# Decay attention, then two MLPs, on one core: the inverted row sums transposed into the banks of the value products, and ScalarE copying all four groups of transposed probabilities

## The chip, the cores and the metric

One core of one Trainium2 chip runs the whole kernel in one launch. The metric is the device time in microseconds (us), the median of three runs. Engines are named as in the profile: PE is TensorE (PEld its weight loads), DVE VectorE, ACT ScalarE, POOL GpSimd, SP the queue that issues most DMAs. Each engine works through its own queue in program order, so an instruction that waits holds up everything queued behind it on that engine.

## What is computed

Causal attention with a decay bias over 4 x 8 heads, 576 tokens, head size 64, and two MLPs behind it on the 2304 tokens:

```python
scores = scale * np.matmul(q, k.transpose(0, 1, 3, 2))
cum = np.cumsum(np.maximum(s, 0.0), axis=-1)
bias = -(cum[:, :, :, None] - cum[:, :, None, :])
scores = np.where(causal, -1000000000.0, scores + np.minimum(bias, 0.0))
scores = scores - np.max(scores, axis=-1, keepdims=True)
attn = np.exp(scores)
attn = attn / (np.sum(attn, axis=-1, keepdims=True) + 1e-09)
x = np.matmul(attn, v)                      # rearranged to 2304 x 512
x = np.maximum(x @ moe_w_in, 0.0) ** 2 @ moe_w_out
h = np.maximum(np.maximum(x @ w1, x @ w2), x @ w3)
return h @ moe2_w_out
```

## The kernel before

**Attention.** The 32 heads are worked in 16 pairs; the two heads of a pair sit in the two halves of the 128 partitions. Each pair has NU = 9 *units* u = 0 to 8: units 0 to 7 are 64-row blocks of queries (two units share a matmul group of 128 query rows, and unit u has (u // 2 + 1) x 128 keys), unit 8 is the tail of 64 queries with 576 keys. Units 0 to 3 are window w = 0, units 4 to 8 window w = 1. A unit goes through these steps:

- `s` (u_s, PE): scores of a pair of units into one of two score tiles; `max` (u_max, DVE): adds the causal bound, takes the negated maximum; `exp` (u_exp, ACT): exponentials, with the row sums accumulated into `sums[p, w]`.
- `t` (u_t, PE, L727): 64 x 64 transposes of the probabilities into a tile of `ring_t`; done at odd units (units 1 and 3 share a tile) and at unit 8, so there are four groups, here t3, t5, t7 and t8.
- `et` (u_et): each group is copied to SBUF: et3 (L754), et5 and et7 (L756) by ACT, et8 (L759) by DVE.
- `pv` (w_pv, PE, L779): the value products of a window into another tile of `ring_t`; pv0 needs et3, pv1 needs et5, et7 and et8. `out0`/`out1` (w_out_, DVE, L787) copies the product to SBUF.
- `rc` (w_rc, DVE, L695 and L696): adds 1e-9 to the window's sums and inverts them. Two small transposes (PE, L734) bring them into columns 448 to 511 of the tile of t5 (window 0) or t8 (window 1), and `cp` (w_cp, DVE, L690) copies them out.
- `keep` (SP, L702, L704) stores these rows in DRAM, `rows` (SP, L711) reads them back broadcast over 64 partitions, `px` (POOL, L792) multiplies, `xst` (SP, L797) stores the result in `x_at`.

`ring_t` has two tiles of two banks, taken in turn: t3, t5 and t7 of a pair fall on one, pv1 of the pair before, pv0 and t8 on the other. So t7 waits until t5's tile has been read, t8 until pv0's has, and pv1 until t8's has.

**The order of the work.** `attention()` runs a step number n over all 144 units; in each step it goes through ORDER and does operation `op` for unit n + d. The list is the order of each engine's queue. `pump` starts or continues the preparation of MLP weights (loads L392 on SP; L397 to L408 on DVE; L415 and L433 on POOL; L429 on ACT) in six of nine steps. Before the operations of a step come the loads of later pairs: k, q and the cumulated sums at unit 7, v at unit 6 of a pair. In step numbers modulo 9, PE's queue is

```
t7 s2 t8 [sums of w=1] s4 t3(u=1) s6 pv1 t3(u=3) s8 t5 [sums of w=0] s0(next pair) pv0
```

where t7, t8 and pv1 belong to the pair before the one whose scores are being made.

**The MLPs.** `experts()` follows on the same queues. The first MLP goes over eight blocks of the hidden dimension per visit of a token chunk: h products (L810), relu, square and a split into two parts (ACT L973 to L975, DVE L976), and the x products (L997) two blocks behind. For the next chunk it loads `x_at` (SP, L900) and splits it (ACT L802, DVE L805). In this stage the weight loads L392 are issued on POOL.

Of the kernel before, what the change touches and what calls it, by code (L numbers as in the profile page):

```python
# [8 lines left out]
F32 = mybir.dt.float32  # L9
# [40 lines left out]
ST_BUFS = 3  # L50
PACE = 1.5
PACE_ATT = 5
ORDER = [("rc", -2), ("max", 1), ("cp", -3), ("out0", -6), ("out1", -7), ("exp", -1), ("et", -3), ("t", -2), ("s", 2), ("pv", -5), ("rows", -13),
         ("pump", 0), ("keep", -6), ("px", -19), ("xst", -21)]

# [189 lines left out]
def kernel(  # L247
# [15 lines left out]
    nc = tc.nc  # L263
    P = 128
    D = v_tail.shape[2]
# [11 lines left out]
    NU = 2 * SQ // P + 1  # L277
    U0 = 4
# [19 lines left out]
    def psum(at, name, n, shape, side="left"):  # L298
        ps = at.enter_context(tc.tile_pool(name=name, bufs=1, side=side, space=PSUM, reuse_waits="tile"))
        return [ps.tile(shape, F32, name=f"{name}{i}") for i in range(n)]  # L300
# [212 lines left out]
    keep = {i: dram.tile([P, 1024], F32, name="keep_" + "_".join(map(str, i))) for i in second + late}  # L513
# [10 lines left out]
    small = phA.enter_context(tc.tile_pool(name="small", bufs=6))  # L524
# [7 lines left out]
    identF = at1.tile([P, P], F32, name="identF")  # L532
# [16 lines left out]
    def rows(j):  # L549
        return slice(D * j, D * j + D)  # L550
# [68 lines left out]

    NP = MAX_PAIRS or BH // 2  # L620
    units = [(p, u) for p in range(NP) for u in range(NU)]
    wins, ends = {}, {}
    for n, (p, u) in enumerate(units):
        if u in (U0 - 1, NU - 1):
            wins[n] = (p, int(u >= U0))
        if u in (U0 + 1, NU - 1):
            ends[n] = (p, int(u == NU - 1))
    st = {}
    s_t = {}
    t_t = {}  # L630
# [39 lines left out]
    sums = {}  # L670
# [8 lines left out]
        nc.scalar.activation(out=e_u[u][:, 0:w], in_=e_u[u][:, 0:w], func=ACTF.Exp, scale=-1.0, bias=st.pop(n),  # L679
                             accum_out=sums[p, win][:, col:col + 1])  # L680

    tr_t = {}
    rs_t = {}
    rec_t = {}


    def w_cp(p, w):
        nu = U0 + w
        sm = small.tile([NU - U0, P], F32, tag="rec", name="rec", bufs=2)
        nc.vector.tensor_copy(sm[0:nu, :].rearrange("u (h c) -> u h c", c=D), tr_t.pop((p, w)))  # L690
        rec_t[p, w] = sm

    def w_rc(p, w):
        sm = sums[p, w][:, 0:U0 + w]
# [20 lines left out]
    def u_t(n):  # L715
        p, u = units[n]
        b = u // 2
        if u == NU - 1:
            blocks = [(u, k, k) for k in range(NKT)]
        elif u % 2:  # L720
            blocks = [(u - 1 + j, k, (k + (b == 1)) * 2 + j) for k in range(b + 1) for j in range(2)]
        else:
            return
        t = t_t[n] = t_t.pop(n - 2) if u == U0 - 1 else ring_t.take()
        for v, k, at in blocks:
            for h in range(2):
                nc.tensor.transpose(t[:, h, at * D:(at + 1) * D], e_u[v][rows(h), k * P:(k + 1) * P], identF[rows(h), rows(h)])  # L727

        if n in ends:
            _, w = ends[n]  # L730
            o = tr_t[p, w] = t[0:U0 + w, :, 7 * D:8 * D]
            sm = sums.pop((p, w))
            for h in range(2):
                nc.tensor.transpose(o[:, h, :], sm[rows(h), 0:U0 + w], identF[rows(h), rows(h)])  # L734

    et_t = {}

    def u_et(n):
        p, u = units[n]
        if u == U0 - 1:  # L740
            et = et_t[p, 0] = et_p.tile([P, 2, 3, 2, D], F32, tag="et0", name="et0")
            m = 6
        elif u > U0 and (u % 2 or u == NU - 1):
            if u == U0 + 1:
                et_t[p, 1] = et_p.tile([P, NKT, 2, W1 // D, D], F32, tag="et1", name="et1")
            et = et_t[p, 1]
            m = NKT if u == NU - 1 else u + 1
            at = (u - U0) & ~1
        else:
            return  # L750
        t = t_t.pop(n)
        src = t[:, :, 0:m * D]
        if u < U0:
            nc.scalar.copy(out=et.rearrange("p h b j c -> p h (b j c)"), in_=src)  # L754
        elif u < NU - 1:
            nc.scalar.copy(out=et[:, 0:m // 2, :, at:at + 2, :].rearrange("p k j h c -> p h k j c"),  # L756
                           in_=src.rearrange("p h (k j c) -> p h k j c", j=2, c=D))
        else:
            nc.vector.tensor_copy(et[:, :, :, at, :].rearrange("p k j c -> p j k c"),  # L759
                                  src.rearrange("p j (k c) -> p j k c", c=D))  # L760
        ring_t.give(t)

    pvt = {}
# [1 line left out]
    def w_pv(p, w):  # L765
        t = pvt[p, w] = ring_t.take()
        pv = t[:, 0, :]
        xv = hd[p]["xv"]
        et = et_t.pop((p, w))
        last = (2, NKT)[w] - 1  # L770
        for k in range(last + 1):
            kr = ST if k == 4 else P
            f = max(0, k * P - W0 * w)
            for j in range(2):
                if w:
                    rhs = et[0:kr, k, j, f // D:, :]
                else:
                    rhs = (et[:, :, 0:2, j, :] if k == 0 else et[:, :, 2:3, j, :]).rearrange("p h b c -> p b h c")
                nc.tensor.matmul(pv[rows(j), f:(W0, W1)[w]], lhsT=xv[0:kr, j, k, :], rhs=rhs, start=(k == 0), stop=(k == last))  # L779

    ax_t = {}

    def w_out_(p, w):
        t = pvt.pop((p, w))
        n = (W0, W1)[w]
        x = ax_t[p, w] = ax_p.tile([P, W1], F32, tag="ax", name="ax")
        nc.vector.tensor_copy(x[:, 0:n], t[:, 0, 0:n])  # L787
        ring_t.give(t)

    def w_px(p, w):  # L790
# [28 lines left out]
    def first_split(kk, step):  # L819
        t0, n = chunks1[0]  # L820
        if step == 0:
            fx[kk] = fx_p.tile([P, 512], F32, tag="fx", name="fx")[:, 0:n]
            nc.sync.dma_start(out=fx[kk], in_=x_at[kk, :, t0:t0 + n])
        elif step == 1:
            first_x[kk] = tuple(slots_a[-1 - kk][:, i, :] for i in range(2))
            high(fx[kk], first_x[kk][0][:, 0:n])
        else:
            low_of(fx[kk], first_x[kk][0][:, 0:n], first_x[kk][1][:, 0:n])

    def first_products():  # L830
        for m in range(PRE):
            yield from h_products(banks[m], first_x, chunks1[0][1], slots.get(("in", m)))

    def attention():
        setup()
        for f in loads(1):
            f()
        N = len(units)
        fns = dict(s=u_s, t=u_t, max=u_max, et=u_et, exp=u_exp)
        efn = dict(cp=w_cp)  # L840
        wfn = dict(rc=w_rc, pv=w_pv, out0=w_out_, out1=w_out_, keep=w_keep, rows=w_rows, px=w_px, xst=w_xst)
        span = max(abs(d) for _, d in ORDER)
        pre = first_products()
        coming = {}
        for n in range(-span, N + span + 1):
            if 0 <= n < N:
                p = n // NU
                for back in range(3):
                    if p + 2 - back < NP and p >= back:
                        to = p + 2 - back  # L850
                        if n == (to - 2) * NU + LOADS[0]:
                            coming[to] = loads(to)
                        for at, f in zip(LOADS, coming.get(to, ())):
                            if n == (to - 2) * NU + at:
                                f()
            for op, d in ORDER:
                if op == "pump":
                    if PUMP_FROM <= n < N + PUMP_END and n % NU in PUMP_U and (slots.free or slots.open):
                        slots.pump(1)
                elif op in efn:  # L860
                    if n + d in ends:
                        efn[op](*ends[n + d])
                elif op in wfn:
                    if n + d in wins and op not in ("out1", "out0")[wins[n + d][1]]:
                        wfn[op](*wins[n + d])
                elif 0 <= n + d < N:
                    fns[op](n + d)
            if n == N - PRE_AT:
                phQ.close()
                banks.extend(psum(ctx, "first", 2, [P, 512]))  # L870
            for kk in range(KD):
                for step, off in enumerate((-8, 0, 1)):
                    if n == N - PRE_X[kk] + off:
                        first_split(kk, step)
            if n >= N - PRE_AT:
                for _ in range(PRE_N):
                    next(pre, None)
        for _ in pre:
            pass
# [277 lines left out]
    with tc.manual_schedule():  # L1157
        attention()
        phA.close()
        phP.close()  # L1160
        banks.extend(psum(ctx, "banks", 6, [P, 512], "right"))
        if not ONLY_ATT:
            experts()
# [55 lines left out]
```

## Time and profile before

| | |
|---|---|
| time, median of 3 runs | 858.42 us (858.33 to 860.21) |
| the profiled execution: its time / its span | 858.48 us / 856.7 us |
| busy over the span | PE 97%, PEld 82%, DVE 63%, ACT 47%, POOL 18% |
| attention, 40 to 170 us: busy of 130 us | PE 118.3, DVE 105.3, ACT 100.0, POOL 40.9 |
| one pair of heads in attention, from one t7 to the next | 10.36 us where nothing else disturbs it |
| MLPs, from about 188 us to the end | PE busy throughout |

The span is what the profiler records of one execution; the time lies 1.8 us above it. Rows are read as: start and length in us, engine, line, operation, tile written <- tile read, and in square brackets how long the engine stood idle before it and what ended that.

### The profile page before, as it was taken

Reading aid. Unit: us, or ns where it says so; the run is one execution under the profiler, and the core shown is the slowest. Engines: PE = TensorE matmul, PEld = TensorE weight load, DVE = VectorE, ACT = ScalarE, POOL = GpSimd, SP = SyncE. Lnnn points to the kernel's source line nnn. Section 1 sums busy time; section 2 is a strip of 40 time slices with the busy share of each in tenths; the row PEclk is TensorE's granted clock in tenths of the full one; section 3 lists DMA queues with packets and bytes.
Section 4 is the critical chain, followed back from the end, with each engine's and each line's share of the span. In section 5 each row is a group of like instructions: output and inputs, shape, how many; then the busy total and the mean of one; then the engine's idle time right before and its main releaser. Section 6 shows DMA issues by size and latency. Waiting matters only on the chain.

```text
span 856.7 us, 14331 instructions
## 1 busy us (share of the span) xinstructions
PE 827.8 (97%) x5284; PEld 702.1 (82%) x5284; DVE 539.9 (63%) x1119; ACT 401.5 (47%) x817; POOL 155.6 (18%) x237
## 2 busy tenths in 40 slices
PE   5999899899999999999999999999999999999998
PEld 3555555568888889999998888889998899989996
DVE  6787888758885657577677876753464335623442
ACT  5777778764544455445554454442233122421222
POOL 2032323334112332214222314100000000000000
PEclk9999999999999999999999999999999999999999
DMA  4555556635344644698658677719940674026601
GB/s 136 175 157 172 185 179 184 190 98 182 109 174 140 222 168 142 235 394 281 204 190 306 227 268 252 249 74 390 405 152 13 208 249 144 14 74 198 244 1 73
DMA packets 72245, 159.75 MB, mean 186 GB/s; under 512 B 11376, under 2 KB 31408, under 8 KB 72176
## 3 DMA queue, kind: packets, MB, share of 16 engines
q1 hardware_dynamic: 56916, 107.45, 37.0%
q0 software_dynamic: 15248, 51.39, 17.4%
q8 instruction: 41, 0.67, 0.3%
q14 instruction: 28, 0.23, 0.1%
q10 hardware_dynamic: 12, 0.01, 0.0%
HBM read 113.53 MB, written 45.27 MB: 185 GB/s over the span
## 4 chain that ended last, share of the span: by engine, by line
PE 91%; DVE 4%; ACT 2%; DMA 2%; issue 1%; SPq 0%; ACTq 0%; DVEq 0%
PE banks L997 23%; PE banks L1134 13%; PE first L810 12%; PE banks L810 12%; PE banks L1106 9%; PE first L1134 8%; PE pairs L779 4%; PE pairs L727 4%; PE pair L642 2%; PE pairs L642 2%; ACT et L756 1%; PE pair L649 1%; PE pairs L649 1%; DVE e L665 1%; DVE hh L805 1%
## 5 line engine op out<-in xcount | busy, mean ns | idle before, releaser
L997 PE MATMUL banks<-hh,sl 128*128 128x512 f32 (+1 forms) x960 | 209.9, 367 | 0.0
L997 PEld LDWEIGHTS banks<-hh,sl 128*128 128x128 f32 x960 | 175.2, 188 | 22.6
L1134 PE MATMUL banks<-xs,sl 128*128 128x384 f32 x702 | 131.2, 335 | 0.0
L1134 PEld LDWEIGHTS banks<-xs,sl 128*128 128x128 f32 x702 | 122.8, 188 | 0.9 <-DMA sl<-keep_p 0.2
L976 DVE TENSOR_TENSOR hh<-r,hh 128x512 fp32r<-128x512 f32 (+1 forms) x80 | 52.0, 651 | 98.4 <-ACT hh L975 98.2
L810 PE MATMUL first<-xs,sl 128*128 128x512 f32 (+1 forms) x432 | 93.6, 365 | 0.0
L810 PE MATMUL banks<-xs,sl 128*128 128x512 f32 (+1 forms) x432 | 93.6, 365 | 0.0
L679 ACT ACTIVATE e<-e,nm 128x128 f32<-128x128 f32 (+2 forms) x144 | 83.3, 582 | 15.6 <-DVE nm L665 15.2
L810 PEld LDWEIGHTS first<-xs,sl 128*128 128x128 f32 x432 | 78.6, 188 | 9.4
L810 PEld LDWEIGHTS banks<-xs,sl 128*128 128x128 f32 x432 | 78.6, 188 | 9.4
L1134 PE MATMUL first<-xs,sl 128*128 128x384 f32 x432 | 84.6, 335 | 0.3 <-DMA sl<-keep_p 0.3
L1106 PE MATMUL banks<-sl,hh 128*128 128x512 f32 (+1 forms) x342 | 78.4, 382 | 1.9 <-DVE hh L805 1.5
L1134 PEld LDWEIGHTS first<-xs,sl 128*128 128x128 f32 x432 | 75.8, 188 | 0.9 <-issue 0.6
L1106 PEld LDWEIGHTS banks<-sl,hh 128*128 128x128 f32 x342 | 61.4, 188 | 15.9 <-DVE hh L805 3.4
L973 ACT ACTIVATE r<-banks 128x512 f32<-128x512 f32 (+1 forms) x40 | 22.2, 556 | 95.0 <-PE banks L810 91.5
L973 ACT ACTIVATE r<-first 128x512 f32<-128x512 f32 (+1 forms) x40 | 22.2, 556 | 90.7 <-PE first L810 90.7
L727 PEld LDWEIGHTS pairs<-identF,e 64*128 64x128 f32 x800 | 34.0, 141 | 28.1 <-ACT et L756 20.9
L727 PE MATMUL pairs<-identF,e 64*128 64x64 f32 x800 | 41.8, 232 | 14.2 <-ACT et L756 14.2
L1035 ACT COPY s<-first 128x384 f32<-128x384 f32 x36 | 17.2, 479 | 79.3 <-PE first L1134 79.2
L779 PEld LDWEIGHTS pairs<-et,xv 128*64 128x64 f32 (+1 forms) x448 | 27.8, 135 | 31.2 <-issue 5.9
L779 PE MATMUL pairs<-et,xv 128*64 128x320 f32 (+4 forms) x448 | 52.7, 367 | 0.0
L1035 ACT COPY s<-banks 128x384 f32<-128x384 f32 x45 | 21.6, 479 | 57.5 <-PE banks L1134 56.7
(105 smaller groups left out, 1155.5 us busy)
## 6 DMA issues: line engine op xcount, KB each, us to landing
sl<-keep_p SPq DMA_DIRECT2D x68, 512.0 KB
st<-in_w_dram POOLq DMA_DIRECT2D x36, 256.0 KB, 6.0
st<-in_w_out_dram POOLq DMA_DIRECT2D x35, 256.0 KB, 3.8
sl<-keep_out SPq DMA_DIRECT2D x14, 512.0 KB
keep_p<-hi POOLq DMA_DIRECT2D x9, 768.0 KB, 4.9
keep_p<-sums POOLq DMA_DIRECT2D x9, 768.0 KB, 6.5
st<-in_w_in_dram POOLq DMA_DIRECT2D x22, 256.0 KB, 4.1
xr<-x_at SPq DMA_DIRECT2D x20, 256.0 KB
```

What stands on the lines that cost most here:

```text
L642: nc.tensor.matmul(b[:, j, 0:w], lhsT=d["xq"][rows(j), w - P:w], rhs=d["xk"][rows(j), 0:w], start=True, stop=False)
L649: nc.tensor.matmul(b[rows(j), i, 0:hi - lo], lhsT=d["xq"][rows(j), SQ:S], rhs=d["xk"][rows(j), lo:hi], start=True, stop=False)
L679: nc.scalar.activation(out=e_u[u][:, 0:w], in_=e_u[u][:, 0:w], func=ACTF.Exp, scale=-1.0, bias=st.pop(n), accum_out=sums[p, win][:, col:co ...
L727: nc.tensor.transpose(t[:, h, at * D:(at + 1) * D], e_u[v][rows(h), k * P:(k + 1) * P], identF[rows(h), rows(h)])
L779: nc.tensor.matmul(pv[rows(j), f:(W0, W1)[w]], lhsT=xv[0:kr, j, k, :], rhs=rhs, start=(k == 0), stop=(k == last))
L810: nc.tensor.matmul(hps[:, 0:n], lhsT=w[:, wp, kk * P:(kk + 1) * P], rhs=x[kk][xp][:, 0:n], start=(kk == 0 and c == 0), stop=(kk == KD - 1 ...
L973: nc.scalar.activation(out=r[:, 0:n], in_=hps[:, 0:n], func=ACTF.Relu)
L976: nc.vector.tensor_tensor(out=hh[:, 1, 0:n], in0=r[:, 0:n], in1=f32(hh[:, 0, 0:n]), op=ALU.subtract)
L997: nc.tensor.matmul(xacc[d][:, 0:n], lhsT=w[:, wp, d * P:(d + 1) * P], rhs=hh[:, xp, 0:n], start=(m == 0 and c == 0), stop=(end and c == 2))
L1035: nc.scalar.copy(out=x, in_=bank[:, 0:T2])
L1106: nc.tensor.matmul(b, lhsT=hh[g, t][:, hp_, q, h, :], rhs=w[:, wp, lo:hi], start=(begin and n == h == c == 0), stop=(end and n == len(f) - ...
L1134: nc.tensor.matmul(at[m, b][:, 0:T2], lhsT=w[:, wp, at_w + kk * P:at_w + (kk + 1) * P], rhs=x[:, kk, xp, :], start=(i in (0, 1, 3) and kk ...
```

## The change

Three things move. The transposes of the inverted sums leave u_t and stand at the end of w_pv, into columns 448 to 511 of the tile of the value products; `cp` disappears as a step and its copy follows `out` in w_out_. The copy of the fourth group (et8) goes from DVE to ACT. In ORDER `rc` goes two steps later and behind `max`, and `keep`, `rows`, `px` and `xst` go two steps later. The buffers of the copied sums (`rec`) go from 2 to 4.

```diff
-ORDER = [("rc", -2), ("max", 1), ("cp", -3), ("out0", -6), ("out1", -7), ("exp", -1), ("et", -3), ("t", -2), ("s", 2), ("pv", -5), ("rows", -13),
-         ("pump", 0), ("keep", -6), ("px", -19), ("xst", -21)]
+ORDER = [("max", 1), ("rc", -4), ("out0", -6), ("out1", -7), ("exp", -1), ("et", -3), ("t", -2), ("s", 2), ("pv", -5), ("rows", -15),
+         ("pump", 0), ("keep", -8), ("px", -21), ("xst", -23)]
...
-    def w_cp(p, w):
-        nu = U0 + w
-        sm = small.tile([NU - U0, P], F32, tag="rec", name="rec", bufs=2)
-        nc.vector.tensor_copy(sm[0:nu, :].rearrange("u (h c) -> u h c", c=D), tr_t.pop((p, w)))
-        rec_t[p, w] = sm
...
-        if n in ends:
-            _, w = ends[n]
-            o = tr_t[p, w] = t[0:U0 + w, :, 7 * D:8 * D]
-            sm = sums.pop((p, w))
-            for h in range(2):
-                nc.tensor.transpose(o[:, h, :], sm[rows(h), 0:U0 + w], identF[rows(h), rows(h)])
...
-            nc.vector.tensor_copy(et[:, :, :, at, :].rearrange("p k j c -> p j k c"),
-                                  src.rearrange("p j (k c) -> p j k c", c=D))
+            nc.scalar.copy(out=et[:, :, :, at, :].rearrange("p k j c -> p j k c"),
+                           in_=src.rearrange("p j (k c) -> p j k c", c=D))
...
                 nc.tensor.matmul(pv[rows(j), f:(W0, W1)[w]], lhsT=xv[0:kr, j, k, :], rhs=rhs, start=(k == 0), stop=(k == last))
+        sm = sums.pop((p, w))
+        for h in range(2):
+            nc.tensor.transpose(t[0:U0 + w, h, 7 * D:8 * D], sm[rows(h), 0:U0 + w], identF[rows(h), rows(h)])
...
         nc.vector.tensor_copy(x[:, 0:n], t[:, 0, 0:n])
+        sm = rec_t[p, w] = small.tile([NU - U0, P], F32, tag="rec", name="rec", bufs=4)
+        nc.vector.tensor_copy(sm[0:U0 + w, :].rearrange("u (h c) -> u h c", c=D), t[0:U0 + w, :, 7 * D:8 * D])
         ring_t.give(t)
```

## Rows read from the trace of the kernel before

**Rows 1.** The page's head.

```profile
span 856.7 us, 14331 instructions
```

**Rows 2.** Busy us (instructions) in a stretch: PE, PEld, DVE, ACT, POOL; clock; DMA; GB/s.

```profile
40.00:170.00 130.00, 118.32 (x1436) 70.66 (x1432) 105.34 (x363) 99.99 (x268) 40.89 (x42) 0.99 0.59 177
```

**Rows 3.** Waits, 10 to 190 us: who waited for whom: total us, times, longest.

```profile
PE pairs L727 <- ACT et L756: 14.2, 15, 1.7
...
ACT et L754 <- PE pairs L727: 18.6, 15, 1.8
...
ACT et L756 <- DVE rec L690: 10.8, 14, 1.4
```

**Rows 4.** Timeline of one pair that nothing else disturbs.

```profile
71.14 0.71 PE L727 MATMUL pairs<-identF,e 64*128 64x64 f32 x16 [0.69 <-ACT et L756]
...
79.19 0.76 DVE L665 CUSTOM_DVE_ANT_0 e<-pairs,bound_l 128x576 f32<-128x576 f32 x1 [0.88 <-PE pairs L652]
...
79.94 0.87 PE L779 MATMUL pairs<-et,xv 128*64 128x256 f32 x8
...
80.29 0.27 DVE L690 COPY rec<-pairs 4x128 f32<-4x128 f32 x1
...
80.65 0.80 ACT L756 COPY et<-pairs 128x768 f32<-128x768 f32 x1 [0.66 <-DVE rec L690]
...
80.91 0.42 DVE L787 COPY ax<-pairs 128x256 f32<-128x256 f32 x1
...
81.50 0.71 PE L727 MATMUL pairs<-identF,e 64*128 64x64 f32 x16 [0.69 <-ACT et L756]
...
82.65 0.47 PE L727 MATMUL pairs<-identF,e 64*128 64x64 f32 x10
...
83.40 0.40 ACT L679 ACTIVATE e<-e,nm 128x128 f32<-128x128 f32 x1
...
83.75 0.80 DVE L759 COPY et<-pairs 128x640 f32<-128x640 f32 x1
...
85.28 2.42 PE L779 MATMUL pairs<-et,xv 128*64 128x320 f32 x20
```

**Rows 5.** Groups by line and shape: count | busy, mean ns.

```profile
L695 DVE TENSOR_SCALAR sm<-sm 128x4 f32<-128x4 f32 x16 | 8.3, 517 | 0.0
...
L696 DVE RECIPROCAL sm<-sm 128x4 f32<-128x4 f32 x16 | 2.9, 178 | 0.6
```

**Rows 6.** Timeline: one of the sums' instructions beside POOL.

```profile
86.95 1.23 POOL L415 TENSOR_TENSOR wa<-st 128x512 f32<-128x512 f32 x1
...
87.20 1.01 DVE L695 TENSOR_SCALAR sm<-sm 128x4 f32<-128x4 f32 x1
```

**Rows 7.** The same view behind the longest of these waits; 0.66 is the clock.

```profile
156.00:161.00 5.00, 4.31 (x46) 3.30 (x48) 3.08 (x12) 4.21 (x12) 0.04 (x1) 0.66 0.59 189
```

**Rows 8.** Timeline of SP's queue: a window-1 keep and the next one.

```profile
77.46 0.62 SPq L702 DMA_DIRECT2D r<-rec  x1
...
87.17 0.62 SPq L702 DMA_DIRECT2D r<-rec  x1
```

**Rows 9.** Timeline from attention's last value products to x product 3.

```profile
186.36 1.08 SPq L711 DMA_DIRECT2D px<-r  x2
...
188.22 0.49 DVE L787 COPY ax<-pairs 128x320 f32<-128x320 f32 x1 [4.89 <-PE pairs L779]
...
189.71 0.93 POOL L792 TENSOR_TENSOR ax<-ax,px 128x320 f32<-128x320 f32 x1 [1.16 <-DMA px<-r]
...
191.10 4.58 SPq L900 DMA_DIRECT2D xr<-x_at  x6
...
198.31 0.43 DVE L397 TENSOR_SCALAR wa<-st 128x512 uint32<-128x512 uint32 x1 [1.92 <-DMA xr<-x_at]
...
202.37 1.78 DVE L976 TENSOR_TENSOR hh<-r,hh 128x512 fp32r<-128x512 f32 x1
...
207.13 2.88 PE L997 MATMUL banks<-hh,sl 128*128 128x512 f32 x12
```

More of the change, by code (lines that the diff above doesn't have):

```diff
@@ L621 @@
     units = [(p, u) for p in range(NP) for u in range(NU)]
-    wins, ends = {}, {}
+    wins = {}
     for n, (p, u) in enumerate(units):
@@ L625 @@
             wins[n] = (p, int(u >= U0))
-        if u in (U0 + 1, NU - 1):
-            ends[n] = (p, int(u == NU - 1))
     st = {}
@@ L680, in u_exp @@
                              accum_out=sums[p, win][:, col:col + 1])
-    tr_t = {}
     rs_t = {}
     rec_t = {}
-    def w_cp(p, w):
-        nu = U0 + w
-        sm = small.tile([NU - U0, P], F32, tag="rec", name="rec", bufs=2)
-        nc.vector.tensor_copy(sm[0:nu, :].rearrange("u (h c) -> u h c", c=D), tr_t.pop((p, w)))
-        rec_t[p, w] = sm
     def w_rc(p, w):
@@ L839, in attention @@
         fns = dict(s=u_s, t=u_t, max=u_max, et=u_et, exp=u_exp)
-        efn = dict(cp=w_cp)
         wfn = dict(rc=w_rc, pv=w_pv, out0=w_out_, out1=w_out_, keep=w_keep, rows=w_rows, px=w_px, xst=w_xst)
@@ L859, in attention @@
                         slots.pump(1)
-                elif op in efn:
-                    if n + d in ends:
-                        efn[op](*ends[n + d])
                 elif op in wfn:
```

## Prediction

> **What bounds the kernel now.** The page's head gives the span, 856.7 us [rows 1]. The table of busy time by stretch comes next: from 40 to 170 us, in attention, PE is busy 118.3 of 130 us, DVE 105.3 and ACT 100.0 [rows 2]. PE is the bound, but it idles for nearly a tenth of this stage, while both helpers have room on average. In the MLPs PE never idles, so what attention loses or wins arrives at the end unless the handover changes it.
>
> The list of waits says what PE idles for: one thing, 14.2 us in 15 waits of the transposes L727 for a copy by ACT [rows 3]. ACT's copy has waited in turn, 10.8 us in 14 times, for DVE's copy of the transposed sums, cp (L690) [rows 3]. One undisturbed pair on the timeline shows the chain [rows 4]. cp0 starts on DVE at 80.29. Behind it ACT starts et5 at 80.65, after idling 0.66 us. et5 takes 0.80, and t7 starts at 81.50, after PE has idled 0.69. The reason is the tile: cp and et5 read the same banks, cp stands first in ORDER, and ACT's read is kept behind DVE's. t7 takes that tile again, so PE pays for a 5 x 128 copy that it doesn't need. The pair lasts from 71.14 to 81.50, 10.36 us [rows 4]; without the stall it would last 9.67.
>
> **Part 1: the sums leave the tile of t5 (gain).** et5 then waits for t5 and for ACT's own queue only. ACT was ready 0.66 us before it started, at 79.99, so et5 ends at 80.79 and t7 could start at 80.84. PE itself is done with pv0 at 80.81 (79.94 + 0.87) [rows 4]. PE and ACT arrive together, so the whole of ACT's wait is gained: **-10.8 us** [rows 3]. What stays of the 14.2 is 3.4, from pairs in which ACT had a weight cast or a split in front of et5. The bounds of this term are -14.2 (everything) and -8 (a quarter of the waits is met by something else in ACT's queue).
>
> The clock adds to it. Behind the longest wait, 1.7 us [rows 3], the granted clock of 156 to 161 us was 0.66 of full speed on average [rows 7], so part of it was spent at 1.2 instead of 2.4 GHz. 5 x (1 - 0.66) = 1.7 us of PE's work were lost. I count **-1.7 us**, since that wait shrinks to about 0.6; the bounds are 0 and -1.7.
>
> **Part 2: the transposes behind pv, cp behind out (cost).** PE makes the same four small transposes per pair, only later, so they cost nothing by themselves. They wait for rc, though, and t7 is queued behind those of window 0. And t8 takes the tile that pv0 used, so it now waits for out0 and then cp0. In the undisturbed pair max of unit 8 ends on DVE at 79.95; rc0 takes 0.52 + 0.18 on average [rows 5] and ends at 80.65, before pv0 ends at 80.81. Then two maxima come, out0 and cp0. out0 began at 80.91 in the old order; cp0 (0.27) leaves from in front of it and rc0 (0.70) comes in: 81.34. With 0.42 for out0 and 0.27 for cp0, t8's tile is free at about 82.03. t8 follows t7 by 1.15 (82.65 - 81.50), so it wants to start at 80.87 + 1.15 = 82.02. On average there is nothing to spare, and a DVE weight operation in this place becomes a stall of PE. The old trace shows how much of that there is: 15 undisturbed waits of 0.69 are 10.35 us, and the other 3.85 of the 14.2 came from such operations in front of cp0 and from ACT's. I take 2.5 of these 3.85 as returning at t8: **+2.5 us**. The lower bound is 0. The upper one comes from the one row in which POOL was at work: L695 lasted 1.01 us, until 88.21, and POOL's operation ended at 88.18 [rows 6]. If that happened in every pair (0.5 more than the mean), the term would be 3.85 + 15 x 0.5 = 11.
>
> The Trainium skill, in "SBUF — State Buffer", section "SBUF: two separate sides", calls the port pair that DVE and GpSimd share an exclusive lock that one instruction holds to its end while the other blocks; the row agrees to 0.03 us, and by that rule rc0 is late wherever it meets a POOL operation.
>
> **Part 3: et8 from DVE to ACT (nothing).** It takes 0.80 from DVE [rows 4]. On ACT it costs at most 0.80, what the larger copy of 128 x 768 takes there. What hides it is ACT's idle time in front of et3, 18.6 us in 15 waits, 1.24 a pair [rows 3]. In its place it follows an exponential of 0.40 at 83.40, so it ends at about 84.6, and pv1, which reads it, starts at 85.28 [rows 4]: 0.7 to spare. Without that cover it costs up to 0.8 a pair, 12 us. For DVE it is 0.80 less in front of the next maxima; rc of window 1 no longer holds the queue for the exponential of unit 8 either. I book no gain for these, as PE isn't waiting for those maxima.
>
> **Part 4: keep, rows, px and xst two steps later.** Inside the stage the distances are kept: seven steps from keep to rows, six to px, two to xst. The products' buffers are held two steps longer, 16 or 17 of 27. SP needs a look: from one window-1 keep at 77.46 to the next at 87.17 its 15 rows follow each other with gaps of about 0.1 us or less, so it issues for 9.7 us per pair with one weight load among them [rows 8]. A pair of 9.7 to 9.9 us is what SP can just serve. It may lag, but k, q and v are loaded about a pair ahead, so I book nothing.
>
> At the end of attention the moves do show. Today the last sums are stored and read back before the last value products are done: out1 at 188.22, px at 189.71, and SP issues the first load of the next chunk's x at 191.10, 2.9 us after out1 [rows 9]. In the new order the last sums are transposed only behind these products. The chain from there is out1 0.49, cp1 0.27, two stores to issue (0.62 each [rows 8]) 1.3, their landing, the two reads 1.1, landing, px 0.93, and 0.5 for xst. For a landing the rows have 189.71 - 187.44 = 2.3 [rows 9], which I take for both. The sum is 9.2 us: everything queued behind this chain on SP (the loads of x) and on POOL (weight loads) is 6.3 us later against PE. DVE stands at L397 until 198.31, waiting for a transfer, and from there works through to hh of block 3 (L976), 202.37 to 204.15; x product 3 starts at 207.13 [rows 9]. The slack is 3.0, and 6.3 - 3.0 = 3.3 us of PE stall would follow if nothing gave. L976 took 1.78 there, so DVE was being held up by neighbours that will be elsewhere. I take **+2.0 us**; the bounds are 0, and 5 if the clock falls as in [rows 7].
>
> **Sum.** The profiled execution took 858.48 us, 1.8 over its span, and equals the median of the runs, 858.42. 858.5 - 10.8 - 1.7 + 2.5 + 2.0 = **850.5 us**.
>
> **The rivals.**
> - *The full gain.* DVE, rid of et8, keeps up at t8, and the handover is hidden by slack further on: 858.5 - 10.8 - 1.7 = 846.0. For it: DVE has 25 idle us in 130 [rows 2]. Against: the 0.0 to spare at t8. Chance 0.13.
> - *The stall moves to rc0.* POOL's px meets rc0 in every pair, and the transposes of the sums hold PE in front of t7, then cp0 holds t8. With 0.5 more per pair (7.5, of which 2.5 is in the forecast): 855.5. For it: a mean of 0.52 for an operation on 128 x 4 elements says that it already meets POOL often [rows 5]. Against: a part of the wait falls under pv0. Chance 0.12. The lock in the skill's page named above is this mechanism.
> - *SP sets the pair.* With two weight loads in a pair SP issues for about 10.3 us, the old pair; if its lag grows past the pair by which it runs ahead, k, q and v come late and the time stays near 858.5. For it: the gapless rows [rows 8]. Against: most pairs have fewer loads, and the lag must pile up over many. Chance 0.13.
> - *ACT is late with et8 (slower).* Place: pv1 behind et8, in each pair. It costs nothing up to 0.7 us of delay; to end above 861 it has to take 10.6 us, 0.7 more in each of 15 pairs, so et8 must end 1.4 us later than worked out. For it: ACT is busy 100 of 130 us [rows 2] and gets weight casts of its own in this place. Against: its 1.24 idle us per pair. Price 861 to 864; chance 0.12.
>
> **How the numbers follow.** The forecast has 0.50, and its own range is 847 to 854, from its terms' nearer bounds. The range for 8 in 10 goes from 845.5, just under the full gain, to 858, where SP's case ends. A measurement tells a change of about 0.3%, 2.6 us, from none. Faster than 855.8: the forecast 0.50, the full gain 0.13, and 0.11 of rc0's 0.12, in all 0.74. Within 0.3%: the rest of that and SP's case, 0.14. Slower: ACT's case, 0.12.
>
> **What the next profile would show.** If part 1 is right, the wait of ACT's L756 for L690's successor is gone, and t7's wait is under 0.2 us in undisturbed pairs, which last 9.7 to 9.9 us. If part 2 is, some t8 wait for DVE's copy of the sums, 2 to 3 us in all. If part 3 is, et3 still waits for PE, about 0.5 us a pair. If part 4 is, the first load of x is issued about 9 us behind the last out1, and PE has a gap of about 2 us near x product 3. The prediction is wrong if t7 still waits as long, now for the small transposes behind pv0; if pv1 waits for ACT; or if the handover costs more than 5 us, with the clock at its lower level.

## The result, and the profile after

862.28 us (median of 9 runs, 861.06 to 866.30) against 858.33 (9 runs, 856.86 to 860.96): the ratio is 1.0052, with a 95% interval of 1.0034 to 1.0070. The change makes the kernel slower by half a per cent. 850.5 had been predicted.

The page's head, and below it the busy time by stretch in early attention (columns as in [rows 2]):

```profile
span 859.2 us, 14421 instructions
...
20.00:40.00 20.00, 20.00 (x246) 11.75 (x244) 14.87 (x62) 17.03 (x47) 1.67 (x2) 1.00 0.60 187
40.00:60.00 20.00, 20.00 (x246) 11.96 (x244) 15.06 (x59) 18.10 (x50) 8.04 (x8) 1.00 0.54 151
60.00:80.00 20.00, 20.00 (x242) 11.47 (x238) 16.84 (x62) 17.66 (x49) 5.00 (x6) 1.00 0.55 176
```

From 20 to 80 us PE does not idle at all. One pair of this stretch on the timeline of the changed kernel (t is now L719, pv L764, the sums' transposes L767, et5 L741, et8 L744, out L775, cp L777, rc L687 and L688):

```profile
85.00 0.87 PE L764 MATMUL pairs<-et,xv 128*64 128x256 f32 x8
85.02 0.78 ACT L741 COPY et<-pairs 128x768 f32<-128x768 f32 x1
85.24 0.15 DVE L687 TENSOR_SCALAR sm<-sm 128x4 f32<-128x4 f32 x1
...
85.86 0.71 PE L719 MATMUL pairs<-identF,e 64*128 64x64 f32 x16
86.52 0.42 DVE L775 COPY ax<-pairs 128x256 f32<-128x256 f32 x1
86.86 0.27 DVE L777 COPY rec<-pairs 4x128 f32<-4x128 f32 x1
...
87.27 0.53 PE L719 MATMUL pairs<-identF,e 64*128 64x64 f32 x10
...
88.17 0.68 ACT L744 COPY et<-pairs 128x640 f32<-128x640 f32 x1
...
89.84 2.42 PE L764 MATMUL pairs<-et,xv 128*64 128x320 f32 x20
```

Against [rows 4]: et5 runs while pv0 does, t7 follows pv0 without a gap, cp0 ends at 87.13 just before t8 at 87.27, and et8 is done at 88.85, 1 us before pv1. Such a pair lasts 9.60 us (pv0 starts at 46.60, 56.20, 65.80 and 75.40) where it lasted 10.36. By pv0 of the tenth pair the kernel is at 104.93, where the one before was at 111.97: 7.0 us ahead.

There the gain ends. The waits of PE up to 260 us in the changed kernel (who waited for whom: total us, times, longest):

```profile
PE pairs L719 <- ACT et L741: 5.3, 4, 2.7
...
PE banks L983 <- DVE hh L962: 3.7, 1, 3.7
PE pair L640 <- DMA xq<-in_qT_dram: 1.5, 1, 1.5
```

The old wait (14.2 us in 15 [rows 3]) has shrunk to four, and two new ones stand beside it. All of them but one t7 wait of 0.35 us (at 96.18) lie behind 110 us. The timeline shows what the first two kinds wait for; SPq rows are issues of DMAs by SP:

```profile
110.95 0.43 SPq L600 DMA_DIRECT2D xq<-in_qT_dram  x1
...
115.82 0.49 PE L640 MATMUL pair<-xk,xq 64*128 64x128 f32 x4 [1.55 <-DMA xq<-in_qT_dram]
...
135.26 0.40 SPq L813 DMA_DIRECT2D fx<-x_at  x1
...
138.18 0.62 ACT L792 CAST sl<-fx 128x512 fp32r<-128x512 f32 x1 [2.21 <-DMA fx<-x_at]
...
140.13 0.78 ACT L741 COPY et<-pairs 128x768 f32<-128x768 f32 x1
...
140.96 0.87 PE L719 MATMUL pairs<-identF,e 64*128 64x64 f32 x16 [2.67 <-ACT et L741]
```

At 115.82 PE waits for q, which SP issued at 110.95. At 138.18 ACT stands in front of a cast of x rows (fx, the first chunk of the MLP, read back from what xst stored), which SP issued at 135.26; et5 is queued behind that cast, and t7 behind et5. Twice more ACT does so (0.36 and 1.04), with t7 waits of 0.82 and 1.49. Both kinds are loads of SP's queue that come late. The granted clock falls behind two of these waits, and once more at the end of attention (the third row):

```profile
118.00:122.00 4.00, 4.00 (x38) 2.70 (x36) 1.80 (x8) 3.31 (x8) 0.85 (x2) 0.64 0.52 165
...
142.00:146.00 4.00, 4.00 (x32) 2.20 (x30) 1.93 (x9) 3.73 (x11) 1.70 (x3) 0.66 0.89 225
200.00:220.00 20.00, 16.27 (x60) 12.87 (x59) 16.35 (x26) 8.67 (x15) 7.90 (x11) 0.83 0.39 138
```

From pv0 of the tenth pair to that of the last, the changed kernel takes 68.0 us (104.93 to 172.96) and the one before 65.6 (111.97 to 177.52). The 7.0 us have become 4.6, and 4.3 at the last out1 (183.92 against 188.22 [rows 9]). PE's part of this second half, first in the kernel before, then in the changed one:

```profile
111.97:177.52 65.55, 59.30 (x706) 35.34 (x703) 54.16 (x185) 50.43 (x134) 21.69 (x22) 0.97 0.59 177
...
104.93:172.96 68.03, 61.37 (x706) 36.55 (x702) 48.82 (x179) 53.79 (x141) 21.71 (x22) 0.95 0.61 180
```

PE idled 6.3 us before (65.55 - 59.30) and idles 6.7 now: the new waits have taken the place of the old one. The other 2.1 us are a longer busy time of the same 706 instructions, at a mean clock of 0.95 against 0.97.

SP's queue explains why. How far SP lags can be read from its load of k for the next pair but one, which stands behind the scores of unit 8 in program order: up to 36 us it is issued as these end, then 0.4, 1.2, 3.6, 3.6, 4.1, 4.9, 6.2 and 6.9 us later. In the kernel before this lag went up and down between 0.4 and 3.3 from the fifth pair on. The starts of these loads, and the weight loads L392 that SP issues between one and the next:

| | start of the k load, us | to the next, us, with weight loads in brackets |
|---|---|---|
| before | 58.96 | 11.8 (3), 10.0 (0), 9.7 (1), 10.8 (2), 11.7 (3), 10.1 (0), 9.7 (1), 11.9 (2), 12.1 (2) |
| after | 56.61 | 12.1 (3), 9.6 (0), 10.0 (1), 10.7 (2), 11.4 (3), 10.3 (0), 10.7 (1), 11.2 (2), 12.5 (2) |

Over these nine pairs SP needs 10.84 us a pair before (58.96 to 156.53) and 10.94 after (56.61 to 155.09). Rows of one of them in the changed kernel, from a k load to the next:

```profile
78.25 0.54 SPq L596 DMA_DIRECT2D xk<-in_kT_dram  x1
78.83 0.43 SPq L600 DMA_DIRECT2D xq<-in_qT_dram  x1
79.36 0.87 SPq L607 DMA_DIRECT2D ck<-c_dram  x2
80.28 0.58 SPq L607 DMA_DIRECT2D cq<-c_dram  x2
80.90 0.36 SPq L392 DMA_DIRECT2D st<-in_w_out_dram  x1
81.36 0.65 SPq L694 DMA_DIRECT2D r<-rec  x1
...
87.54 0.64 SPq L615 DMA_DIRECT2D xv<-in_v_tail_dram  x1
88.27 0.54 SPq L596 DMA_DIRECT2D xk<-in_kT_dram  x1
```

This pair holds one weight load and takes 10.02 us; 8.80 of it are issues, and no pause among its rows is longer than 0.2. A PE pair of 9.60 us is shorter than that. The gain of the first half was taken out of SP's lead over PE, and when the lead was used up SP set the pace, about as slow as the pairs had been. In the kernel before, no wait for q or x rows stands between 100 and 180 us: SP just kept up there.

At the end of attention the rows that answer to [rows 9]:

```profile
183.92 0.49 DVE L775 COPY ax<-pairs 128x320 f32<-128x320 f32 x1 [8.30 <-PE pairs L767]
...
191.67 0.88 POOL L782 TENSOR_TENSOR ax<-ax,px 128x320 f32<-128x320 f32 x1 [0.95 <-DMA px<-r]
...
193.00 4.48 SPq L886 DMA_DIRECT2D xr<-x_at  x6
...
204.98 1.89 DVE L962 TENSOR_TENSOR hh<-r,hh 128x512 fp32r<-128x512 f32 x1
...
206.92 5.06 PE L983 MATMUL banks<-hh,sl 128*128 128x512 f32 x11 [3.73 <-DVE hh L962]
```

SP issues the first load of x 9.1 us behind the last out1 (2.9 before). PE stands for 3.73 us in front of x product 3, which then takes 5.06 us (2.88 before); the clock of 200 to 220 us was 0.83. From the last out1 to the span's end it is 675.3 us (859.2 - 183.92), and 668.5 before (856.7 - 188.22): the handover costs 6.8. So 4.3 gained and 6.8 lost make the span 2.5 longer; the medians differ by 3.95.

### The profile page after: what moved, and what is told of

It is laid out like the page before. It is cut to its first block, busy times and chain, and to the rows that moved or that the text cites. A ratio compares the mean times of both kernels' runs of the same rounds, so it can differ in the third digit from the quotient of the medians.

```text
span 859.2 us, 14421 instructions
## 1 busy us (share of the span) xinstructions
PE 833.7 (97%) x5284; PEld 705.3 (82%) x5284; DVE 523.3 (61%) x1103; ACT 408.9 (48%) x833; POOL 154.7 (18%) x237
## 4 chain that ended last, share of the span: by engine, by line
PE 89%; DMA 4%; DVE 3%; ACT 2%; SPq 1%; issue 1%; POOL 0%; DVEq 0%; ACTq 0%; POOLq 0%
PE banks L983 22%; PE banks L1120 13%; PE first L800 11%; PE banks L800 11%; PE banks L1092 9%; PE first L1120 8%; PE pairs L764 5%; PE pairs L719 3%; PE pairs L640 2%; PE pair L640 2%; PE pair L647 1%; DMA st<-in_w_in_dram 1%; DMA fx<-x_at 1%; PE pairs L647 1%; ACT e L677 1%
## 5 line engine op out<-in xcount | busy, mean ns | idle before, releaser
L983 PE MATMUL banks<-hh,sl 128*128 128x512 f32 (+1 forms) x960 | 212.4, 370 | 3.7 <-DVE hh L962 3.7
L764 PEld LDWEIGHTS pairs<-et,xv 128*64 128x64 f32 (+1 forms) x448 | 27.8, 135 | 31.0 <-ACT e L677 8.9
L764 PE MATMUL pairs<-et,xv 128*64 128x320 f32 (+4 forms) x448 | 52.7, 367 | 0.0
L782 POOL TENSOR_TENSOR ax<-ax,px 128x256 f32<-128x256 f32 (+1 forms) x32 | 26.6, 831 | 126.1 <-DMA px<-r 106.2
L719 PEld LDWEIGHTS pairs<-identF,e 64*128 64x128 f32 x800 | 34.7, 143 | 17.1 <-ACT et L741 7.6
```

Of the source, the lines that this page charges most:

```text
L782: nc.gpsimd.tensor_tensor(out=x[:, 0:n], in0=x[:, 0:n], in1=rs_t.pop((p, w))[:, 0:n], op=ALU.mult)
L983: nc.tensor.matmul(xacc[d][:, 0:n], lhsT=w[:, wp, d * P:(d + 1) * P], rhs=hh[:, xp, 0:n], start=(m == 0 and c == 0), stop=(end and c == 2))
```

## The experiments

All times are compared with runs of the kernel before on the same chip, whose medians lie between 857.6 and 858.6; a difference between two edited kernels, many of which ran on different chips, can carry that 1 us.

**One half of the change each.** First the kernel before with only et8 on ACT, then the changed kernel with et8 back on DVE (the same edit the other way round):

```diff
-            nc.vector.tensor_copy(et[:, :, :, at, :].rearrange("p k j c -> p j k c"),
-                                  src.rearrange("p j (k c) -> p j k c", c=D))
+            nc.scalar.copy(out=et[:, :, :, at, :].rearrange("p k j c -> p j k c"),
+                           in_=src.rearrange("p j (k c) -> p j k c", c=D))
```

> The kernel before with one edit: ACT instead of DVE copies the fourth group of transposed probabilities (et8). If ACT hides this copy, as the prediction said, the time is 858.3 within 1.5 us, et3 still waits for PE, and pv1 doesn't wait for ACT. If the fuller ACT queue is what made the changed kernel slower (its long waits stand at ACT's copies), this kernel is slower by 3 us or more, and t7 waits longer than the 14.2 us of before.

> The changed kernel with the fourth copy back on DVE: only the move of the sums and of the later steps. If the loss comes from SP's queue in attention and from the end of attention, as the traces suggest, it stays at 862 within 2 us, and pairs last 9.6 to 9.9 us until SP is late. If ACT's copy is the cause, it is at 858 or below.

Measured: 859.42 us, ratio 1.0004 (0.9990 to 1.0019), and 861.39 us, 1.0029 (1.0014 to 1.0045). With et8 on ACT alone, t7 waits as ever, 13.8 us in 15. Without it the waits are those of the whole change: t7 6.9 us in 4, q 1.8, x product 3 3.5. Moving et8 costs nothing and gains nothing that can be measured; the loss lies in the sums and their steps.

**The last window the old way.** Only the last pair's window 1 has its sums transposed behind t8 again and its keep, rows, px and xst two steps earlier:

```diff
...
+            if n == N + 1:
+                w_rc(*LAST)
+            if n == N + 2:
+                w_cp(*LAST)
             for op, d in ORDER:
+                if op in ("keep", "rows", "px", "xst") and n + d + 2 == N - 1:
+                    wfn[op](*LAST)
...
```

> The changed kernel, but the sums of the last pair's window 1 go the old way (transposed behind t8, copied before et8, stored, read and multiplied two steps earlier). If the chain of store, read and multiplication behind the last value products costs what the two traces show at the handover (6.8 us between the start of h block 2 and the end: 675.6 against 668.8), the time falls by 5 to 7 us to 855 to 857, and PE has no gap at x product 3. If that gap only moves further on, or the loss sits in attention alone, it falls by less than 2 us.

Measured: 856.71 us, 0.9980 (0.9965 to 0.9994), a further single run of it 855.21. No wait of PE is left at the handover, and 5.6 us come back; t7's four waits (5.7 us) and those for q remain. From the last out1 to the end it takes 668.7 us there (854.7 - 185.99, shown below), as in the kernel before (668.5). The handover's cost is shown, and it is this chain.

**Work taken off SP.** xst is issued by POOL, which makes its input:

```diff
-        nc.sync.dma_start(out=x_at[h // 2, :, b * S + lo:b * S + hi], in_=ax_t.pop((p, w))[:, 0:hi - lo])
+        nc.gpsimd.dma_start(out=x_at[h // 2, :, b * S + lo:b * S + hi], in_=ax_t.pop((p, w))[:, 0:hi - lo])
```

> The changed kernel, but the stores of the attention's output (xst, two per pair, about 1 us of SP's queue with the gaps) are issued by POOL right where it has multiplied. If SP's lag makes q and the first MLP's x arrive late, the pairs stay at 9.6 to 9.8 us to the end of attention, the waits for q and for x disappear, and 4 to 7 us are gained there, 1 to 3 more at the handover, where SP's loads no longer stand behind POOL: 853 to 857. If SP isn't the cause, the time stays within 2 us of 862.

> The kernel before, with the stores of the attention's output issued by POOL. If SP's queue only becomes a limit with pairs of 9.6 us, nothing is gained where pairs take 10.4 us: 858.4 within 1.5 us. If SP was a limit before already, it is 2 us or more faster.

In the changed kernel: 854.48 us, 0.9949 (0.9929 to 0.9969), 7.8 below the change. The wait for q is gone; t7 still waits 6.6 us in 4, nearly all at casts of x rows. Where the gain lies is read from the last out1: with the early last window alone, with xst on POOL alone, and with both (a version that follows below):

```profile
185.99 0.49 DVE L788 COPY ax<-pairs 128x320 f32<-128x320 f32 x1 [5.63 <-PE pairs L778]
...
183.32 0.49 DVE L775 COPY ax<-pairs 128x320 f32<-128x320 f32 x1 [8.62 <-PE pairs L767]
...
180.03 0.49 DVE L788 COPY ax<-pairs 128x320 f32<-128x320 f32 x1 [5.63 <-PE pairs L778]
```

With xst on POOL alone out1 comes at 183.32, only 0.6 us earlier than in the change; from there to the end it takes 670.8 us (854.1 - 183.32) instead of 675.3. In this profile, taken of the longest of four runs (856.1 us), most of the gain lies at the handover, where SP issues the first load of x 4.7 us behind out1 instead of 9.1. So these 7.8 us by themselves don't show what the stores cost attention; that comes with both cures.

In the kernel before: 862.32 us, 1.0048 (1.0023 to 1.0074), where 858.4 was expected. That expectation was missed: issued by POOL, the stores cost 4.0 us there. At 40.34 t7 waits 1.63 us (1.09 in the same pair of the kernel before), the clock of 40 to 44 us is 0.60, and that pair lasts 12.9 us; how POOL's stores bring this about isn't shown. SP is no bound there: its k loads stand 0.02 us or less behind the scores of unit 8 in all pairs but the last. Relief of SP is worth something only in the changed kernel.

The Trainium skill, "DMA: Bandwidth & Descriptors", section "Issuing engines are not separate DMA queues", says that spreading DMAs over several engines brings no bandwidth and only saves issue time. Here the issue time was what ran short: 8.80 of 10.02 us in the pair shown above.

**The x rows earlier.** The loads of fx stand 15 instead of 8 steps ahead of their casts:

```diff
-    enumerate((-8, 0, 1))
+    enumerate((-15, 0, 1))
```

> The changed kernel, but the four loads of the first MLP's x are put into SP's queue 15 instead of 8 steps before ACT's cast of them. If ACT's waits for these loads (2.2, 0.4 and 1.0 us) and with them t7's waits of 2.7, 0.8 and 1.5 us come from SP's lag of some 6 us, they shrink to 0.8 or less (the cast itself still stands in front of et5), and with the clock that fell behind the longest, 3 to 5 us are gained: 857 to 859. If they come from ACT's own load, nothing changes: 862.

Measured: 861.19 us, 1.0024 (1.0008 to 1.0040): one us, not 3 to 5. t7's waits fall to 0.5 us, but PE now waits for q, 1.90 and 2.27 us, and the handover's gap stays (3.3). SP's lag wasn't shortened, it only hit another load.

**Both cures, and all three.**

> The last pair's window 1 the old way and the stores on POOL, together. If handover and SP's queue are separate losses, the gains add, less what the stores already gave at the handover: 854.5 less 3 to 4, 850 to 852. If they are one loss, it stays at 854.

> All three: the last pair's window 1 the old way, the stores on POOL, the loads of the first MLP's x earlier. If the three named losses are what kept the change from its gain, this one has the prediction's attention: t7's waits together under 4 us, no gap at the handover, 845 to 849. If something else limits the pairs, it stays above 850.

With the early last window and xst on POOL: 849.29 us, 0.9890 (0.9869 to 0.9910), better than both kernels and 13.0 below the change; apart the two cures gave 5.6 and 7.8, in all 13.4, though by their profiles they gained in part at the same place, the handover, so that the sum fits is partly chance. Against the early last window alone (856.71, and 855.21) the stores on POOL are worth 5.9 to 7.4 us, and this is attention: the last out1 comes at 180.03 instead of 185.99, and the rest takes 668.4 us (848.4 - 180.03) as against 668.7. With fx early too: 851.06, 0.9908 (0.9880 to 0.9935), which can't be told from it; 845 to 849 had been expected. What PE waits for up to 260 us in the better one, the start of the kernel left out:

```profile
PE pairs L725 <- ACT et L755: 4.9, 3, 2.2
...
PE pairs L733 <- DVE sm L694: 1.2, 2, 0.7
```

The second line is rc0. One of its two waits, with its cause on the timeline:

```profile
94.30 1.27 POOL L433 TENSOR_TENSOR sl<-wa,sl 128x512 fp32r<-128x512 f32 x1
94.40 1.21 DVE L693 TENSOR_SCALAR sm<-sm 128x4 f32<-128x4 f32 x1
...
95.87 0.22 PE L733 MATMUL pairs<-identF,sm 64*4 64x64 f32 x2 [0.70 <-DVE sm L694]
```

DVE's operation ended at 95.61, POOL's at 95.57, and 0.15 is its length when alone (85.24 above).

**A dose of SP's queue.** If issuing on SP sets the pace, a further DMA there must cost its length. In window 1 the first store of the sums is issued twice; in the first three kernels to the same place:

```diff
         if w:
+            nc.sync.dma_start(out=d[:, 0:W0].rearrange("j (u c) -> u j c", c=P), in_=sm[0:U0, :])
             nc.sync.dma_start(out=d[:, W0:W1], in_=sm[U0:nu, :].rearrange("o (j c) -> o j c", c=D))
```

> One dose of the suspected cost: in each window 1 SP issues the first store of the sums a second time (same rows, same place), 0.64 us of its queue a pair. If SP's queue is what holds attention from about pair 5 on, the dose is paid in full by the ten or eleven pairs in which SP already lags: 862.3 + 6 to 8 = 868 to 870 us, with longer waits for q and for the x rows. If SP's lag is only a bystander (a share of the late loads has another cause), the dose is hidden: within 1 us of 862.3.

> The same dose in the kernel before, whose pairs last 10.4 us while SP issues for 9.7: by the theory of SP's queue about 0.7 of free time a pair swallow it, so within 1.5 us of 858.4, at most 2 more from the pairs with two weight loads. If a further store on SP costs by itself what it costs in the changed kernel (a rival: the store, not the queue), it is 6 to 8 us here too.

> The same dose in the version with the early last window and with POOL issuing the stores of x (849.3). There SP has lost 0.34 us twice a pair, so it issues for about 9.0 to 9.3 in a pair of 9.6 to 9.9; the dose brings it to about 9.9. By the theory it costs something between nothing and the 7 us that xst's removal won: about 2 to 4, 851 to 853. If SP no longer matters there, within 1 us of 849.3.

Measured: 886.54 us, 1.0335 (1.0314 to 1.0357); 884.20 us, 1.0303 (1.0280 to 1.0326); 874.57 us, 1.0192 (1.0177 to 1.0208). All three lost 24 to 27 us, far outside every expectation. The dose was spoiled: SP's rows between 95 and 118 us show it standing 1.1 to 2.3 us in front of the second store, which writes where the first has just written, so the dose was 1.7 to 2.9 us a pair instead of 0.6. Next, four places of their own in turn for the second stores:

```diff
+    r_dram.append([dram.tile([2, W1], F32, name=f"rx{i}") for i in range(4)])
...
+            nc.sync.dma_start(out=r_dram[2][p % 4][:, 0:W0].rearrange("j (u c) -> u j c", c=P), in_=sm[0:U0, :])
```

> In the three runs before, the second store had the same place as the first and SP stood still until the first had landed: about 1.1 to 2 us more than its own 0.64. Here it goes to four places of its own in turn, so it costs SP 0.65 to 0.75 us a pair and no wait. If SP's queue holds attention from about pair 5 on, ten or eleven pairs pay the dose: 862.3 + 6 to 8 = 868 to 870 us. If SP's lag is a bystander: within 1 us of 862.3.

> The same dose without the wait in the kernel before, which has about 0.7 us a pair free on SP: by the theory of SP's queue within 1.5 us of 858.4 (up to 2 more from pairs with two weight loads). If a store costs time by itself wherever it stands, 6 to 8 us here as well.

> The same dose without the wait in the version with the early last window and POOL's stores of x (849.3). SP issues there for about 9.0 to 9.3 us in pairs of 9.6 to 9.9, so the dose brings it back to the pair's length: 0 to 4 us, 849 to 853; by the rival (the store itself) 6 to 8, 855 to 857.

Sixteen issues of 0.60 us and a gap of 0.07 are 10.7 us. The changed kernel went to 871.63 us, 1.0145 (1.0124 to 1.0166), 9.4 up; the one before to 862.72, 1.0045 (1.0030 to 1.0060), 4.1 up; the better version to 857.09, 0.9981 (0.9969 to 0.9993), 7.8 up. In the changed kernel the last out1 comes at 193.58, 9.7 us later than without the dose, so it was paid in attention. Its waits up to 260 us:

```profile
PE pairs L721 <- ACT et L743: 7.8, 3, 4.2
...
PE pair L641 <- DMA xq<-in_qT_dram: 4.7, 3, 3.9
PE banks L985 <- DVE hh L964: 4.3, 1, 4.3
```

The same stores cost the changed kernel nearly their full length and the one before less than half, so it is the queue and not the store. The better version alone wouldn't tell them apart: its 7.8 us are what the store by itself was to cost. But over the first nine pairs, in which eight of the sixteen further stores are issued, the dose cost the kernel before nothing (94.8 us from pv0 to pv0 against 94.9) and the better version 0.6 (87.8 against 87.2): where SP has room, such a store costs next to nothing. All three expectations were too low, that for the changed kernel (868 to 870) by 2 us: the kernel before had less to spare on SP than I took it to have (two t7 waits of 2.6 and 2.4 us appear there at casts of x rows), and the better version has next to nothing.

**The weight loads off SP.** In attention POOL issues L392:

```diff
-    queue = [nc.sync]
+    queue = [nc.gpsimd]
```

> The changed kernel with attention's weight loads issued by POOL; the stores of x stay on SP. In the profile SP's queue from the k load at 56.61 us on takes 12.1, 9.6, 10.0, 10.7, 11.4, 10.3, 10.7, 11.2 and 12.5 us a pair, with 3, 0, 1, 2, 3, 0, 1, 2 and 2 weight loads; without them about 9.3. If these loads are what pushes SP over the new pair of 9.6 us, no wait for q or x is left in the later pairs and about 6 to 8 us come back: 854 to 857, with the handover still in it. The rival: POOL waits for its row products' inputs, so loads queued behind them are late and DVE's weight work, and with it PE, waits: 862 or more.

> The same in the kernel before. If SP already set the pace of its second half (its k loads follow each other every 10.8 us from 58.96 on, where an undisturbed pair takes 10.36), 1 to 3 us are gained: 855.5 to 857.5. If SP wasn't its bound, 858.4 within 1.

> Early last window, and weight loads of attention on POOL: the prediction's kernel with both of its sore places gone and the stores of x left on SP. About 849 if the loads are what SP is short of, as with the stores of x on POOL (849.3); 845 to 847 if they relieve SP more than those did; 856 or more if POOL brings them late.

With them ran the repeat of the early last window that was mentioned above (its weight loads stayed on SP), as a level for the last of the three.

> A repeat of the changed kernel with the early last window alone, as the level for the next run: 856.7 within 2.

Measured: 860.50 us, 1.0020 (1.0003 to 1.0037), 1.8 below the change; 861.49, 1.0031 (1.0013 to 1.0049), 3.1 above the kernel before; 854.27, 0.9951 (0.9934 to 0.9968), 1 to 2.4 below the early last window alone. The 6 to 8 us did not come, nor either of the two times expected of the kernel before. SP's rows in the first of the three, from one load of v on:

```profile
90.27 0.63 SPq L615 DMA_DIRECT2D xv<-in_v_tail_dram  x1
91.00 0.68 SPq L596 DMA_DIRECT2D xk<-in_kT_dram  x1
...
93.65 0.64 SPq L694 DMA_DIRECT2D r<-rec  x1
96.33 0.60 SPq L696 DMA_DIRECT2D r<-rec  x1
...
97.70 0.49 PE L640 MATMUL pair<-xk,xq 64*128 64x128 f32 x4 [1.85 <-DMA xq<-in_qT_dram]
...
102.72 0.70 SPq L596 DMA_DIRECT2D xk<-in_kT_dram  x1
```

From the k load at 91.00 to the next SP issues for 8.2 us, yet that takes 11.7: SP stands 2.0 us between the two stores of the sums (L694, L696). The waits of SP's own queue, 40 to 180 us, name what ended this pause:

```profile
SPq L787 <- DMA xk<-in_kT_dram: 5.0, 3, 2.9
...
SPq L696 <- DMA xv<-in_v_tail_dram: 2.0, 1, 2.0
```

It was the landing of the tail of v, issued at 90.27, and that is the eighth DMA before the store. In all 16 waits of SP for a landing in this stretch (12.4 us), and in all 15 of the changed kernel (5.3 us), the DMA waited for is the eighth before. What was saved in issues went into these waits: SP stood 7.1 us longer for landings, about as much as had been expected to come back. Why these landings come later with the weight loads on POOL, and whether the eight belong to the program or to the chip, no run took apart.

## Why the prediction was wrong

- **Part 1 was right**, in mechanism and, as long as SP had a lead, in size: et5 no longer waits for cp, PE doesn't idle for it, and pairs last 9.60 us (9.7 to 9.9 predicted). Over the first nine pairs 7.7 us came in (94.92 from pv0 to pv0 against 87.20), 0.86 a pair; over 15 pairs that would be 12.9, for which -10.8 - 1.7 + 2.5 = -10.0 had been booked.
- **Part 2 was too dear**, harmlessly: PE nowhere waits for cp0 at t8 in the change, where 2.5 us stood. rc's first operation takes 164 ns on average in the new place, 517 in the old [rows 5]. The rival "the stall moves to rc0" fell, but the mechanism exists: with the other waits gone it cost 1.2 us in the better version (95.87 above).
- The Trainium skill, "SBUF — State Buffer", section "SBUF: two separate sides", describes that lock on the port which DVE and GpSimd share. The trace agrees: DVE's operation ended 0.04 us behind POOL's.
- **Part 3 was right**: nothing, 1.0004. The slower rival, ACT late with et8, did not happen; et8 ends 1 us before pv1. The measured time lies in that rival's range (861 to 864) without its mechanism, which is chance.
- **Part 4 failed, and with it the prediction.** The step reads: "A pair of 9.7 to 9.9 us is what SP can just serve. It may lag, but k, q and v are loaded about a pair ahead, so I book nothing." It came from one stretch of 9.7 us [rows 8] with one weight load, and the rival was put at 0.13 because "most pairs have fewer loads". Counted over nine pairs there are 14 loads, 0 to 3 a pair; five of the nine pairs have two or three, and those with two took 10.8 to 12.1 us in the kernel before, where 10.3 had been worked out. SP went 10.84 us a pair in the kernel before with hardly a pause among its rows. So SP was a second bound right behind the first. The first half's 7.0 us were paid from SP's lead over PE: the lag of 4.9 to 6.9 us that its k loads have from 99 to 121 us is nearly as large. The dose (9.4 us in the changed kernel, 4.1 in the one before) and its reverse (5.9 to 7.4 us by POOL's stores, once the handover was cured) show the queue as the cause. That the second half even lost 2.5 us is mostly the lower clock behind the new waits: PE idles about as much as before there, and two stretches of 4 us at a clock of 0.64 and 0.66 are 2.8 us of PE's work where one of 1.7 stood [rows 7].
- **The handover** was right in its chain (9.2 us predicted, 9.1 measured) and mis-sized in the term: +2.0 booked, 6.8 measured, above the bound of 5. The wait was 3.7, as the sum without any give (3.3) had it; the lower clock behind it cost 2.2 in the product alone (5.06 against 2.88). The early last window gave back 5.6.
- Together: the span grew by 2.5 us where a fall of 8.0 was forecast. Of these 10.5 us, 5.7 lie in attention (4.3 gained instead of 10.0) and 4.8 in the handover.

With both cures the time is 849.3 us, close to the 850.5 forecast; but it is another kernel, and agreement there is no merit of the sum.

What stays open: why SP's DMAs land later when the weight loads are on POOL, and how POOL's stores cost the kernel before 4.0 us. The better version isn't free of SP either: its k loads follow each other every 10.0 us over seven pairs (55.01 to 124.91), then 12.0 and 13.3 us in the two pairs that hold the first loads of x rows; no run took the two apart.

## What to carry to other kernels

Before a stall of the bounding engine is booked as a gain for every turn of a loop, ask what the next bound's turn is, averaged over the whole stage and with all that shares its queue, not over one stretch: a DMA-issuing queue without pauses is an engine at its limit. Its pauses count too: look up what they wait for, since a queue that stands for the landing of its own older DMAs doesn't get faster by issuing less. A lead that such a queue has built up pays for the first turns of a faster loop, so a profile whose early part is as predicted and whose late part isn't points to a lag that piles up. When steps are moved later inside a pipeline, write down the last turn's chain separately: there nothing comes behind to hide it.

## What was unexpected of the hardware

- The granted clock does not follow the length of a PE wait alone: it fell to 0.64 behind 1.55 us (115.82) and to 0.66 behind 2.67, but it was 1.00 from 200 to 220 us with a gap of 2.1 (xst on POOL) and with one of 2.8 (weight loads on POOL). What tells these apart was not tried.
- Two stores a pair moved from SP to POOL changed the time by -7.8 us in one kernel and by +4.0 in the other. Such an issue took POOL 0.58 us and SP mostly 0.33 to 0.38.
- When a landing held up SP's queue, it was that of the eighth DMA before, in all 15 such waits of the changed kernel between 40 and 180 us (5.3 us), and in all 16 with the weight loads on POOL (12.4 us). Whether chip or program sets this wasn't tried.
